# The first two attention blocks with queries on partitions, and a float64 conversion whose sign is carried by Prelu

## The chip, the cores and the metric

The kernel runs on one core of a Trainium2 chip. The metric is device time in microseconds (us), the median of several executions. The profile is of one execution; its engines are PE (matrix products), DVE (vector), ACT (scalar functions), POOL, and SP, which here issues the DMAs.

## The reference, cut to what matters

Attention with a causal mask and a bias from cumulated sums, then two feed-forward blocks, the first behind a layer norm and the second behind a mixing of rank 32 along the sequence. Batch 4, 8 heads, sequence S = 576, head size 64, width 512, hidden width 2048. The weights of both feed-forward blocks, U and V come in float64.

```python
# attention, per batch and head
cum  = cumsum(maximum(s, 0), -1)
bias = -(cum[..., :, None] - cum[..., None, :])
scores = where(causal, -1e9, q @ k.T / 8 + minimum(bias, 0))
attn = exp(scores - max(scores)); attn = attn / (sum(attn) + 1e-9)
x = attn @ v                                   # (B, S, 512) over all heads
# first feed-forward block
xn = (x - mean(x)) / sqrt(var(x) + 1e-6) * g_ln
x = x + maximum(xn @ w_ch1, 0) @ w_ch2
# second: mix along the sequence, then feed-forward
u = x + (x.T @ U @ V).T
out = u + maximum(u @ w_ch1b, 0) @ w_ch2b
```

## The kernel before, in words

Rows of the sequence are worked on in blocks: A is queries 0 to 255 and B queries 256 to 575 of a batch; A0 is block A of batch 0, B3 block B of batch 3. For each block attention runs by pairs of heads (class `Pair`, four pairs per block): `load`, `prep` (split into a high and a low part), `score`, `trans` (the probabilities are transposed on PE, copied to a tile `pB`) and `pv`. A0 and A1 (`FULL`) use full float32 and no split. In `score` a matmul with `sel` and `ksum` adds the bias, DVE takes the maximum in the same pass in which it masks (L761), ACT takes the exponential with a running sum (L767, an activation and then a read of its accumulator), a reciprocal follows (L774), and the probabilities are multiplied by it on ACT, DVE or POOL (L780 to L783). `pv` (L846 for the full blocks) has v as the stationary operand, so its result has the head's 64 features on partitions; it is copied into the block's tile x (L374 or L375), 128 features of 512 by 256 queries.

`layer_norm` then works on x with features on partitions: sums over features are products with a tile of ones (L920 and L927), everything else is passes of 128 by 256. Its result is split in `xh` and `xl`, the operands of the feed-forward matmuls. A block of the first feed-forward layer takes 16 steps, each for 128 hidden units (`mlp1` at L1277 to L1279, `mlp2` at L1310 to L1312). Steps 0 to 7 are A0 with the first half of the hidden units, 8 to 15 A1 with the same weights, 16 to 31 both with the second half. 128 such steps are followed by the second layer.

Weights come as pairs of 32-bit words in a raw tile `wr` (four of them). `f64_to_f32` makes float32 of them in four operations: ACT scales the high words (L507), ACT turns the low words into integers (L511), DVE shifts and joins them (L513), DVE puts the sign in from the raw tile (L515). The result is split in a high and a low part. Steps 0 to 7 split into `w` tiles (`w_split`) and write them out; the second half is converted ahead and written out (`w_ahead`, from step `W0`), and is loaded again later; the second layer's weights likewise (`w1_ahead`, `w2_ahead`, from step `W1`).

Order: every operation is handed to a planner (`Plan`) with a priority and an estimated cost for each engine that can do it. The planner simulates the engines and one DMA queue, does four more passes with due times and prices, keeps the shortest, and writes the order out. Buffers of a tag are given out in the order in which they were asked for. `AT` says between which steps a block's attention is asked for, `LN` at which step its layer norm. Until the first matmul of step 0 the planner fills PE's waits with matmuls on ones (L1463, fillers). `setup` loads s, cumulates it and builds `ksum`, the sums relative to the last key of each range, for 128, 256, 384 and 512 keys, and the 576-key sums that go to memory (L433 to L449).

Of the kernel before, what the change touches and what calls it, by code (L numbers as in the profile page):

```python
# [41 lines left out]
def f(ap):  # L42
    return ap.bitcast(F32)
# [285 lines left out]
def mha_ffn_mixer_ffn(ctx: ExitStack, tc, qkv_p, qkv_a, qkv_b, s, g, w1, w2, U, V, out):  # L329
# [70 lines left out]
    COL = [sum(KEYS[:i]) for i in range(5)]  # L400
# [11 lines left out]
    def setup():  # L412
        s_sb, cum = (P.buf("pB", [128, 2, 1344]) for _ in range(2))

        def rel(c0, c1):
            return s_sb.tile.rearrange("p a c -> p (a c)")[:, c0:c1]

        for y in range(4):
            load(PRO, R * S * 4, lambda y=y: nc.sync.dma_start(s_sb[R * y:R * (y + 1), 0, :S], s), [], [(s_sb, "y%d" % y)])
# [9 lines left out]
        def mask(d, n):  # L429
# [3 lines left out]
        dve(PRO, S, lambda: nc.vector.tensor_scalar(out=s_sb[:, 0, :S], in0=s_sb[:, 0, :S], scalar1=0.0, scalar2=8.0, op0=ALU.max, op1=ALU.mult),  # L433
            [s_sb], [s_sb], 0.521)
        dve(PRO, S, lambda: nc.vector.tensor_tensor_scan(cum[:, 0, :S], s_sb[:, 0, :S], s_sb[:, 0, :S], 0.0, ALU.add, ALU.max),
            [s_sb], [cum], 1.042)

        for i in range(5):
            c0, c1 = COL[i], COL[i] + KEYS[i]
            pr = PRO + (i >= 2)  # L440
            dve(pr, KEYS[i], lambda i=i, c0=c0, c1=c1: nc.vector.tensor_scalar(
                out=rel(c0, c1), in0=cum[:, 0, :KEYS[i]], scalar1=cum[:, 0, KEYS[i] - 1:KEYS[i]], scalar2=None, op0=ALU.subtract),
                [cum] + [s_sb] * (i == 0), [s_sb] if i == 0 else [(s_sb, i)], 0.521, 128)
            if i == 4:
# [54 lines left out]
    def f64_to_f32(prio, n, dst, raw, bd, br, words=(0, 1), psum=False):  # L499
# [108 lines left out]
    class Pair:  # L608
# [11 lines left out]
        def load(self, prio, gate):  # L620
# [93 lines left out]
        def score(self, prio, tick):  # L714
# [7 lines left out]
            rd = [qk] if full else [(qk, x) for x in ("raw", "h", "l")] if self.blk == "A" else [(qk, x) for x in ("kh", "kl", "k", "qh", "ql", "z0", "z1", "q0", "q1", "q2")]  # L722
            nt = len(tick)
            nc_ = len(ts) * nt
            sm, rc = (P.buf(tag, [128, 4]) for tag in ("sm", "rc"))
# [18 lines left out]
            else:  # L744
                for x, i in enumerate(tick):
# [13 lines left out]
                    pe(prio - 500, 1.2 * mm_full(K) + mm_cost(K) if full else 4 * mm_cost(K) + 200, mm, rd + [sel, (ksum, i)], [(ps, x) for ps in pss], ts)  # L759
# [73 lines left out]
        def pv(self, prio, z):  # L833
# [10 lines left out]
            def mm_f():  # L844
                for k, (j, o0, o1, c) in enumerate(mms):
# [668 lines left out]
```

## Time and profile before

| | |
|---|---|
| runs | 1067.99, 1072.34, 1072.24 us, median 1072.24 |
| profiled execution | 1071.02 us, span of its instructions 1069.2 us |
| busy share of the span | PE 97%, DVE 66%, ACT 48%, POOL 16% |
| mean granted clock of PE | 0.996 of full speed |
| moved by DMA | 253.58 MB, mean 237 GB/s |

PE's busy time counts the fillers too, and an average over the span mixes stages with different limits. Rows of a view give a group's instructions as count, busy time and mean length of one; a granted clock of 1.00 is 2.4 GHz and 0.50 is 1.2 GHz. Window rows give busy time by engine with the number of instructions in brackets, then the granted clock, the DMA share and GB/s.

### The profile page before, as it was taken

Reading aid. Unit: us, or ns where it says so; the run is one execution under the profiler, and the core shown is the slowest. Engines: PE = TensorE matmul, PEld = TensorE weight load, DVE = VectorE, ACT = ScalarE, POOL = GpSimd, SP = SyncE. Lnnn points to the kernel's source line nnn. Section 1 sums busy time; section 2 is a strip of 40 time slices with the busy share of each in tenths; the row PEclk is TensorE's granted clock in tenths of the full one; section 3 lists DMA queues with packets and bytes.
Section 4 is the critical chain, followed back from the end, with each engine's and each line's share of the span. In section 5 each row is a group of like instructions: output and inputs, shape, how many; then the busy total and the mean of one; then the engine's idle time right before and its main releaser. Section 6 shows DMA issues by size and latency. Waiting matters only on the chain.

```text
span 1069.2 us, 20135 instructions
## 1 busy us (share of the span) xinstructions
PE 1042.1 (97%) x7393; PEld 960.0 (90%) x7393; DVE 709.3 (66%) x1744; ACT 508.5 (48%) x1224; POOL 175.5 (16%) x333
## 2 busy tenths in 40 slices
PE   9998999999999999989999999999999999999998
PEld 6687998999999999979899999999998999899997
DVE  7999978886798766685785533755645744744521
ACT  7988866785676564575664332421211311311211
POOL 1123213241341232211420000200100200200000
PEclk9998999999999999999999999999999999999999
DMA  6999997555954598378349599995474375176483
GB/s 231 356 327 330 335 363 258 187 177 204 324 170 147 187 325 271 122 236 301 113 162 332 194 333 404 340 342 204 149 268 165 109 276 196 54 249 230 138 276 100
DMA packets 98755, 253.58 MB, mean 237 GB/s; under 512 B 16320, under 2 KB 44992, under 8 KB 94304
## 3 DMA queue, kind: packets, MB, share of 16 engines
q1 hardware_dynamic: 98656, 252.28, 68.4%
q8 instruction: 59, 0.97, 0.4%
q14 instruction: 40, 0.33, 0.1%
HBM read 198.69 MB, written 62.99 MB: 245 GB/s over the span
## 4 chain that ended last, share of the span: by engine, by line
PE 70%; DMA 11%; DVE 8%; ACT 6%; issue 2%; SPq 1%; POOL 1%; DVEq 0%; ACTq 0%; POOLq 0%
PE ps L1199 5%; PE ps L1201 5%; PE ps L1200 5%; PE ps L1277 5%; PE ps L1279 4%; PE ps L1278 4%; PE acc L1310 3%; PE acc L1312 3%; PE acc L1311 3%; PE acc L1236 3%; PE acc L1237 3%; PE ps L1236 3%; PE ps L1237 3%; PE acc L1238 3%; PE ps L1238 3%; PE ps L853 3%
## 5 line engine op out<-in xcount | busy, mean ns | idle before, releaser
L1277 PE MATMUL ps<-xh,w 128*128 128x256 f32 (+1 forms) x512 | 160.5, 314 | 3.3 <-DVE mx L761 1.9
L1279 PE MATMUL ps<-xl,w 128*128 128x256 f32 (+1 forms) x512 | 152.5, 298 | 1.2 <-POOL xl L381 1.2
L1278 PE MATMUL ps<-xh,w 128*128 128x256 f32 (+1 forms) x512 | 152.4, 298 | 0.0
L1310 PE MATMUL acc<-hh,w 128*128 128x256 f32 (+1 forms) x448 | 136.6, 305 | 0.5 <-ACT hh L1283 0.5
L1312 PE MATMUL acc<-hl,w 128*128 128x256 f32 (+1 forms) x448 | 130.1, 290 | 0.6 <-DVE hl L1284 0.6
L1284 DVE SCALAR_TENSOR_TENSOR hl<-ps,hh 128x256 fp32r<-128x256 f32 (+1 forms) x144 | 64.6, 449 | 98.6 <-ACT hh L1283 97.9
L1311 PE MATMUL acc<-hh,w 128*128 128x256 f32 (+1 forms) x448 | 129.9, 290 | 0.0
L1283 ACT ACTIVATE hh<-ps 128x256 fp32r<-128x256 f32 (+1 forms) x144 | 57.7, 403 | 118.5 <-PE ps L1279 117.9
L1277 PEld LDWEIGHTS ps<-xh,w 128*128 128x128 f32 x512 | 98.1, 192 | 9.3 <-issue 2.7
L1279 PEld LDWEIGHTS ps<-xl,w 128*128 128x128 f32 x512 | 97.8, 191 | 1.5 <-POOL xl L381 1.5
L1278 PEld LDWEIGHTS ps<-xh,w 128*128 128x128 f32 x512 | 98.2, 192 | 0.7
L767 ACT ACTIVATE t<-t,mx 128x128 f32<-128x128 f32 (+4 forms) x144 | 83.0, 578 | 29.2 <-DVE mx L761 20.9
L1159 ACT ACTIVATE w<-hl 128x256 fp32r<-128x256 f32 x87 | 35.5, 417 | 124.2 <-DVE hl L1179 124.1
L1310 PEld LDWEIGHTS acc<-hh,w 128*128 128x128 f32 x448 | 85.2, 190 | 3.4 <-issue 1.8
L1312 PEld LDWEIGHTS acc<-hl,w 128*128 128x128 f32 x448 | 85.1, 190 | 1.1 <-DVE hl L1284 1.1
L1311 PEld LDWEIGHTS acc<-hh,w 128*128 128x128 f32 x448 | 85.3, 191 | 0.3
L1179 DVE TENSOR_TENSOR hl<-ps,hh 128x256 f32<-128x256 f32 x128 | 48.6, 418 | 45.0 <-PE ps L1201 43.9
L1179 DVE TENSOR_TENSOR hh<-ps,hh 128x256 f32<-128x256 f32 x64 | 27.1, 423 | 73.1 <-ACT hh L374 71.9
L806 PE MATMUL ps<-ident,t 128*128 128x128 f32 x400 | 64.5, 277 | 10.5 <-ACT t L780 3.2
L379 DVE TENSOR_TENSOR pB<-ps,pB 128x512 fp32r<-128x512 f32 (+1 forms) x112 | 62.6, 571 | 14.3 <-ACT pB L374 13.6
L374 ACT ACTIVATE pB<-ps 128x384 fp32r<-128x384 f32 (+3 forms) x115 | 56.5, 500 | 18.7 <-PE ps L806 18.0
L806 PEld LDWEIGHTS ps<-ident,t 128*128 128x128 f32 x400 | 46.3, 140 | 18.9 <-ACT t L780 5.4
(235 smaller groups left out, 2847.9 us busy)
## 6 DMA issues: line engine op xcount, KB each, us to landing
w<-w_dr SPq DMA_DIRECT2D x128, 512.0 KB, 7.4
pB<-w_dr SPq DMA_DIRECT2D x34, 1024.0 KB, 6.2
w_dr<-wr SPq DMA_DIRECT2D x48, 512.0 KB, 4.7
qk<-w_dr SPq DMA_DIRECT2D x26, 768.0 KB, 5.9
wr<-w1a SPq DMA_DIRECT2D x16, 512.0 KB, 5.8
wr<-w2a SPq DMA_DIRECT2D x16, 512.0 KB, 6.4
w_dr<-w SPq DMA_DIRECT2D x16, 512.0 KB, 6.4
wr<-w1b SPq DMA_DIRECT2D x16, 512.0 KB, 6.5
```

The lines of the kernel that those rows point to most:

```text
L767: act(prio, K, lambda t=t, mx=mx, o=o, K=K, x=x, y=nt * z + x: nc.scalar.activation(t[:, o:o + K], t[:, o:o + K], AF.Exp, bias=mx[:, (1 if ...
L806: nc.tensor.transpose(ps[:, 128 * j:128 * (j + 1)], t[:, c:c + 128], ident.tile)
L1179: dve(st - 1000, 256, lambda: nc.vector.tensor_tensor(out=d.tile, in0=region(r), in1=a.tile, op=ALU.add), [p, a], [d])
L1236: nc.tensor.matmul(aa[z].tile, w[:, 0, sl], h[:, 0], start=first, stop=False)
L1237: nc.tensor.matmul(aa[z].tile, w[:, 1, sl], h[:, 0], start=False, stop=False)
L1277: nc.tensor.matmul(ps[:, :n], lhs(k, 0), xh[:, k, :n], start=k == 0, stop=False)
L1278: nc.tensor.matmul(ps[:, :n], lhs(k, 1), xh[:, k, :n], start=False, stop=False)
L1279: nc.tensor.matmul(ps[:, :n], lhs(k, 0), xl[:, k, :n], start=False, stop=k == KT - 1)
L1284: dve(st - 1000, n, lambda: nc.vector.scalar_tensor_tensor(out=hl[:, :n], in0=ps[:, :n], scalar=0.0, in1=f(hh[:, :n]), op0=ALU.max, op1=AL ...
L1310: nc.tensor.matmul(a, w[:, 0, sl], hh[:, :n], start=new, stop=False)
L1311: nc.tensor.matmul(a, w[:, 1, sl], hh[:, :n], start=False, stop=False)
L1312: nc.tensor.matmul(a, w[:, 0, sl], hl[:, :n], start=False, stop=last and (z == 1 or blk == "B"))
```

## The change

For A0 and A1 the product with v is turned (`pv_tok`): the transposed probabilities, now not normalised, are the stationary operand, and v with 64 columns of ones beside it is the moving one. The result has queries on partitions, with the sum of each query's probabilities in the 64 columns beside it. One reciprocal and one multiply normalise it into a tile of 128 queries by 2 by 512. The running sum in the exponential, the pass over the probabilities and the copies of x by head go. The layer norm (`layer_norm_tok`) takes mean and variance along the free axis with statistics operations, scales, and eight transposes bring the normalised x to features on partitions, where g is multiplied in as it is split. x itself is brought to that form later (`x_columns`, at priorities 10 and 18: eight transposes and two copies for each block). `layer_norm` stays for all other blocks.

The tile of q, k, v holds two pairs and the columns of ones; q and k come in one load, v in another. `setup` first loads, cumulates and subtracts only 256 columns; the rest has priority 5. The range of 128 keys is dropped (it uses the 256-key sums). In `f64_to_f32` one Prelu on ACT scales positive words by 2^-112 and negative ones by -2^-80; the three-bit shift that follows moves that difference of exponents into the sign bit, and the sign step on DVE goes. Planner costs of the two ACT steps go from 94 to 135 ns besides the width, and `AT`, `LN`, `W0` and `W1` get other numbers.

```diff
--- before.py
+++ after.py
@@ -32,10 +32,10 @@
 LAST = ("C0", "C1", "C2", "C3", "T0")
 W2SLOTS = 12
 
-AT = {"A2": (6, 9), "A3": (12, 35), "B0": (26, 46), "B1": (48, 63), "B2": (67, 86), "B3": (76, 100)}
-LN = {"A2": 18, "A3": 35, "B0": 55, "B1": 63, "B2": 86, "B3": 100}
-W0 = (4, 12)
-W1 = (16, 66, 50)
+AT = {"A2": (3, 11), "A3": (6, 35), "B0": (24, 46), "B1": (48, 59), "B2": (67, 84), "B3": (78, 98)}
+LN = {"A2": 15, "A3": 35, "B0": 59, "B1": 61, "B2": 84, "B3": 98}
+W0 = (0, 8)
+W1 = (10, 72, 50)
 PASSES = 4
 
...
@@ setup
+        sc, cum = P.buf("xc", [128, 1280]), P.buf("v", [128, 1280])
+        late = 5
+        part = ((0, 256, PRO), (256, S, late))
+
+        for c, (c0, c1, pr) in enumerate(part):
+            for y in range(4):
+                load(pr, R * (c1 - c0) * 4, lambda y=y, c0=c0, c1=c1: nc.sync.dma_start(sc[R * y:R * (y + 1), c0:c1], s[:, c0:c1]), [], [(sc, ("s", c))])
...
+        for c, (c0, c1, pr) in enumerate(part):
+            k = (sc, ("s", c))
+            dve(pr, c1 - c0, lambda c0=c0, c1=c1: nc.vector.tensor_scalar(out=sc[:, c0:c1], in0=sc[:, c0:c1], scalar1=0.0, scalar2=8.0, op0=ALU.max, op1=ALU.mult),
+                [k], [k], 0.521)
+            dve(pr, c1 - c0, lambda c0=c0, c1=c1: nc.vector.tensor_tensor_scan(
+                cum[:, c0:c1], sc[:, c0:c1], sc[:, c0:c1], cum[:, c0 - 1:c0] if c0 else 0.0, ALU.add, ALU.max),
+                [k] + [(cum, 0)] * c, [(cum, c)], 2.084)
+
+        REL = {1: (sc, 576), 2: (sc, 832), 3: (sc, 0), 4: (cum, 640)}
+        for i, (a, c) in REL.items():
             c0, c1 = COL[i], COL[i] + KEYS[i]
-            pr = PRO + (i >= 2)
...
@@ f64_to_f32
-        alts = {"act": (94 + 0.8333 * n, lambda: nc.scalar.activation(dst(), pair(1), AF.Copy, scale=2.0 ** -112))}
...
+        act(prio, n, lambda: nc.scalar.activation(dst(), pair(1), AF.Prelu, scale=2.0 ** -112, alpha=-2.0 ** 32), [(br, words[1])], [bd], 135)
...
-        dv(lambda: nc.vector.scalar_tensor_tensor(out=dst().bitcast(U32), in0=pair(1).bitcast(U32), scalar=0x80000000,
-                                                  in1=dst().bitcast(U32), op0=ALU.bitwise_and, op1=ALU.bitwise_or), [bd, (br, words[1])], [bd])
@@ Pair.load
-                qk = self.qk = self.v = P.buf("qk", [128, 768], dt)
-                load(prio, 512 * 768, lambda: nc.sync.dma_start(qk.tile, qkv_p[b, p]), [], [qk], gate)
+                if p % 2 == 0:
+                    qk = self.qk = P.buf("qk", [128, 2, 832], dt)
+                    P.op(prio, {"pool": (200, lambda: nc.gpsimd.memset(qk[:, :, 768:], 1.0))}, [], [(qk, "one")])
+                else:
+                    qk = self.qk = pairs_of[b, blk][p - 1].qk
+                for c0, c1, key in ((0, 512, "qk"), (512, 768, "v")):
+                    load(prio, 512 * (c1 - c0), lambda c0=c0, c1=c1: nc.sync.dma_start(qk[:, p % 2, c0:c1], qkv_p[b, p, :, c0:c1]), [], [(qk, (key, p % 2))], gate)
...
@@ Pair.score
+                    if full:
+                        act(prio, K, lambda t=t, mx=mx, o=o, K=K, x=x: nc.scalar.activation(
+                            t[:, o:o + K], t[:, o:o + K], AF.Exp, bias=mx[:, x:x + 1], scale=-1.0), [(t, i), (mx, x)], [(t, i)], 160)
+                        continue
...
+            if full:
+                return
...
+        def pv_tok(self, prio):
+
+            b, p, pT, qk = self.b, self.p, self.pT[0], self.qk
+            ps = psum()
+            mms = [(i, z, j) for i in range(2) for z in range(2) for j in range(i + 1)]
+
+            def vv(z, j):
+                c = 512 + 64 * (2 * z + j)
+                a = qk[:, p % 2, c:c + 64]
+                return bass.AP(tensor=a.tensor, offset=a.offset, ap=[a.ap[0], (768 - c, 2), (1, 64)])
+
+            def mm():
+                for k, (i, z, j) in enumerate(mms):
+                    c = 128 * (2 * i + z)
+                    nc.tensor.matmul(ps[:, c:c + 128], pT[:, z, 128 * (i + j):128 * (i + j + 1)], vv(z, j), start=k == 0, stop=k == len(mms) - 1)
+
+            pe(prio - 500, 6 * mm_full(128), mm, [pT, (qk, ("v", p % 2)), (qk, "one")], [ps])
+            if (b, "tok") not in xt:
+                xt[b, "tok"] = P.buf("x", [128, 2, DM])
+            x, sm, rc = xt[b, "tok"], P.buf("sm", [128, 4]), P.buf("rc", [128, 4])
+
+            def reg():
+                return ps.tile.rearrange("p (i z c) -> p i z c", i=2, z=2)
+
+            dve(prio, 4, lambda: nc.vector.tensor_scalar(out=sm.tile, in0=ps.tile.rearrange("p (a c) -> p a c", a=4)[:, :, 64], scalar1=1e-9, scalar2=None, op0=ALU.add),
+                [ps], [sm])
+            dve(prio, 7, lambda: nc.vector.reciprocal(rc.tile, sm.tile), [sm], [rc])
+
+            def norm():
+                r = rc.tile
+                r4 = bass.AP(tensor=r.tensor, offset=r.offset, ap=[r.ap[0], (2, 2), (1, 2), (0, 64)])
+                nc.vector.tensor_tensor(out=x[:, :, 128 * p:128 * (p + 1)].rearrange("p i (z c) -> p i z c", z=2), in0=reg()[..., :64], in1=r4, op=ALU.mult)
+
+            dve(prio, 256, norm, [ps, rc], [(x, p)])
...
+                    if pr.full:
+                        items.append((800, lambda p, g, pr=pr: pr.pv_tok(p)))
+                    for z in () if pr.full else range(2):
...
+    def to_columns(prio, src, reads, k0):
+        ps = psum()
+
+        def tr():
+            for k in range(k0, k0 + 2):
+                for i in range(2):
+                    nc.tensor.transpose(ps[:, 256 * (k - k0) + 128 * i:256 * (k - k0) + 128 * (i + 1)], src(i)[:, 128 * k:128 * (k + 1)], ident.tile)
+
+        pe(prio - 500, 4 * 109, tr, reads + [ident], [ps])
+        return ps
+
+    def layer_norm_tok(prio, b):
+        x, w = xt[b, "tok"], P.buf("ls", [128, 320])
+        n = [P.buf("xs", [128, DM]) for _ in range(2)]
+
+        def st(i, c):
+            return w[:, 12 * i + 6 * c:12 * i + 6 * (c + 1)]
+
+        def col(c):
+            return w[:, 32:36].rearrange("p (i c) -> p i c", i=2)[:, :, c]
+
+        mean, var, y, z = lambda i: w[:, 32 + 2 * i:33 + 2 * i], lambda: col(1), lambda: w[:, 40:42], lambda: w[:, 48:50]
+        for c in range(2):
+            for i in range(2):
+                dve(prio, 256, lambda i=i, c=c: nc.vector.bn_stats(out=st(i, c), in_=x[:, i, 256 * c:256 * (c + 1)]), [(x, 2 * c), (x, 2 * c + 1)], [(w, (i, c))])
+        for i in range(2):
+            dve(prio, 12, lambda i=i: nc.vector.bn_aggr(out=w[:, 32 + 2 * i:34 + 2 * i], in_=w[:, 12 * i:12 * (i + 1)]), [(w, (i, 0)), (w, (i, 1))], [(w, ("mv", i))])
+        mv = [(w, ("mv", i)) for i in range(2)]
+        act(prio, 2, lambda: nc.scalar.activation(y(), var(), AF.Ln, bias=eps.tile), mv + [eps], [(w, "y")], 145)
+        act(prio, 2, lambda: nc.scalar.activation(y(), y(), AF.Exp, scale=-0.5), [(w, "y")], [(w, "y")])
+        dve(prio, 2, lambda: nc.vector.scalar_tensor_tensor(out=z(), in0=var(), scalar=1e-6, in1=y(), op0=ALU.add, op1=ALU.mult), mv + [(w, "y")], [(w, "z")])
+        dve(prio, 2, lambda: nc.vector.tensor_tensor(out=z(), in0=z(), in1=y(), op=ALU.mult), [(w, "y"), (w, "z")], [(w, "z")])
+        dve(prio, 2, lambda: nc.vector.scalar_tensor_tensor(out=y(), in0=z(), scalar=-3.0, in1=y(), op0=ALU.add, op1=ALU.mult), [(w, "y"), (w, "z")], [(w, "y")])
+        for i in range(2):
+            dve(prio, DM, lambda i=i: nc.vector.tensor_scalar(out=n[i].tile, in0=x[:, i], scalar1=mean(i), scalar2=w[:, 40 + i:41 + i], op0=ALU.subtract, op1=ALU.mult),
+                [x, mv[i], (w, "y")], [n[i]], 0.521, 128)
+        xh, xl = P.buf("xh", [128, KT, 320], F32R), P.buf("xl", [128, KT, 320], F32R)
+        for k0 in (0, 2):
+            ps = to_columns(prio, lambda i: n[i], n, k0)
+            for k in range(k0, k0 + 2):
+                def half(k=k, ps=ps, k0=k0):
+                    return ps[:, 256 * (k - k0):256 * (k - k0 + 1)]
+
+                P.op(prio, {
+                    "act": (144 + 0.8333 * 256, lambda k=k, half=half: nc.scalar.activation(xh[:, k, :256], half(), AF.Copy, scale=g_sb[:, k:k + 1])),
+                    "dve": (128 + 1.042 * 256, lambda k=k, half=half: nc.vector.tensor_scalar(out=xh[:, k, :256], in0=half(), scalar1=g_sb[:, k:k + 1], scalar2=None, op0=ALU.mult)),
+                }, [ps, g_sb], [(xh, k)])
+                dve(prio, 256, lambda k=k, half=half: nc.vector.scalar_tensor_tensor(
+                    out=xl[:, k, :256], in0=half(), scalar=g_sb[:, k:k + 1], in1=f(xh[:, k, :256]), op0=ALU.mult, op1=ALU.subtract),
+                    [ps, g_sb, (xh, k)], [(xl, k)], fixed=128)
+        xn[0, b, "A"] = (xh, xl)
+
+    def x_columns(prio, b):
+        t = xt.pop((b, "tok"))
+        x = xt[b, "A"] = P.buf("x", [128, KT, 256])
+        for k0 in (0, 2):
+            ps = to_columns(prio, lambda i: t[:, i], [t], k0)
+            copy(prio, 512, lambda k0=k0: x[:, k0:k0 + 2, :], lambda ps=ps: ps.tile.rearrange("p (k c) -> p k c", k=2), [ps], [(x, k0)], psum=True)
...
-    layer_norm(-50, 0, "A")
+    layer_norm_tok(-50, 0)
     for _, fn in attn_items(1, "A"):
         fn(1, None)
-    layer_norm(4, 1, "A")
+    layer_norm_tok(4, 1)
+    for b in range(2):
+        x_columns(10 + 8 * b, b)
     w_next(0, None)
     w_next(1, None)
     for k in range(2 * WSLOTS):
```

## Rows read from the trace of the kernel before

**Rows 1.** Windows: PE, PEld, DVE, ACT, POOL busy; clock, DMA share, GB/s.

```profile
0.00:9.70 9.70, 8.60 (x54) 6.35 (x54) 5.34 (x14) 4.06 (x10) 1.48 (x8) 1.00 0.70 228
9.70:50.60 40.90, 37.31 (x279) 26.40 (x279) 37.50 (x109) 36.81 (x107) 6.64 (x15) 1.00 0.84 304
50.60:92.20 41.60, 38.70 (x311) 33.86 (x309) 39.87 (x107) 38.61 (x106) 9.03 (x20) 1.00 0.97 337
92.20:126.00 33.80, 31.23 (x248) 29.72 (x248) 31.09 (x78) 28.08 (x76) 11.20 (x20) 0.90 0.92 318
126.00:200.00 74.00, 71.18 (x604) 67.77 (x601) 60.37 (x165) 51.59 (x139) 19.36 (x40) 1.00 0.88 304
200.00:1069.20 869.20, 855.08 (x5910) 795.94 (x5908) 535.09 (x1274) 349.31 (x792) 127.78 (x231) 1.00 0.64 221
```

**Rows 2.** Timeline of PE: start, length, instruction, idle time before it and releaser.

```profile
9.69 0.33 PE L753 MATMUL ps<-ksum,sel 64*128 64x128 f32 x2
...
24.86 2.14 PE L1463 MATMUL acc<-ones 128*128 128x256 bf16 x18
...
50.65 0.36 PE L1277 MATMUL ps<-xh,w 128*128 128x256 f32 x1
...
92.23 0.58 PE L1277 MATMUL ps<-xh,w 128*128 128x256 f32 x1 [0.55 <-ACT xh L374]
```

**Rows 3.** The fillers' line: count, length in ns, first and last start.

```profile
L1463 PE MATMUL acc<-ones x173: 272/273/418, 1.1 to 50.6; 128*128 128x256 bf16 x173
```

**Rows 4.** One window, columns as in Rows 1.

```profile
90.00:100.00 10.00, 7.85 (x39) 7.22 (x40) 9.56 (x20) 8.77 (x25) 6.81 (x11) 0.66 0.85 310
```

**Rows 5.** Groups on DVE, 9.7 to 92.2 us: count, busy us, mean ns.

```profile
L515 DVE SCALAR_TENSOR_TENSOR ps<-wr,ps 128x512 uint32<-128x512 uint32 x21 | 14.2, 687 | 0.1
...
L940 DVE TENSOR_TENSOR xc<-x,ps 128x256 f32<-128x256 f32 x8 | 2.8, 415 | 0.0
L375 DVE CAST w<-ps 128x512 fp32r<-128x512 f32 x4 | 2.8, 688 | 0.1
...
L963 DVE SCALAR_TENSOR_TENSOR xc<-xc,g_sb,ls 128x256 f32<-128x256 f32 x4 | 1.7, 477 | 0.0
L774 DVE RECIPROCAL rc<-sm 128x4 f32<-128x4 f32 x9 | 1.6, 173 | 0.6 <-POOL sm L772 0.4
```

**Rows 6.** Groups on ACT, the same stretch.

```profile
L767 ACT ACTIVATION_READ_ACCUMULATOR t<-t,mx 128x1 f32 x40 | 7.6, 190 | 0.0
...
L374 ACT ACTIVATE x<-ps 64x256 f32<-64x256 f32 x15 | 5.6, 370 | 1.3 <-PE ps L846 1.1
...
L780 ACT ACTIVATE t<-t,rc 128x256 f32<-128x256 f32 x8 | 3.9, 495 | 0.0
...
L780 ACT ACTIVATE t<-t,rc 128x128 f32<-128x128 f32 x7 | 2.5, 392 | 0.0
```

**Rows 7.** Timeline of DVE, in setup and in A0's layer norm.

```profile
4.21 0.46 DVE L433 TENSOR_SCALAR pB<-pB 128x576 f32<-128x576 f32 x1 [3.16 <-DMA pB<-s]
...
4.70 1.36 DVE L435 TENSOR_TENSOR_SCAN pB<-pB 128x576 f32<-128x576 f32 x1
...
40.63 1.41 DVE L940 TENSOR_TENSOR xc<-x,ps 128x256 f32<-128x256 f32 x4
```

**Rows 8.** Pieces of the chain that ended last: start, length, what.

```profile
57.00 0.33 PE ps L806 x3
...
78.04 1.46 PE ps L846 x8
```

**Rows 9.** Waits, SP's queue to 200 us and PE's: total us, times, longest.

```profile
SPq L524 <- DVE ps L515: 16.2, 8, 6.7
...
PE ps L757 <- DMA qk<-qkv_p: 1.2, 2, 0.9
```

**Rows 10.** Timeline of ACT at the start.

```profile
0.75 1.28 ACT L1466 ACT_TABLE_LOAD   x1 [0.75 <-PEq L1507]
```

**Rows 11.** Issues of second-layer w1 loads: length ns, first and last start.

```profile
L524 SPq DMA_DIRECT2D wr<-w1b x16: 327/437/947, 153.0 to 655.3; - x16
```

More of the change, by code (lines that the diff above doesn't have):

```diff
@@ L399, in mha_ffn_mixer_ffn @@
     KEYS = [min(128 * (i + 1), S) for i in range(5)]
-    COL = [sum(KEYS[:i]) for i in range(5)]
+    COL = [sum(KEYS[1:i]) for i in range(5)]
+    COL[0] = COL[1]
     ksum = fixed("ksum", [128, COL[4]], F32R)
@@ new lines, in setup, with rel @@
+        REL = {1: (sc, 576), 2: (sc, 832), 3: (sc, 0), 4: (cum, 640)}
+        for i, (a, c) in REL.items():
+            c0, c1 = COL[i], COL[i] + KEYS[i]
+            pr = PRO if i == 1 else late
+            key = [(a, ("s", y)) for y in range(2)] if i == 3 else [(a, 10 + i)]
+            def rel(y0=0, y1=4, a=a, c=c, i=i):
+                return a[R * y0:R * y1, c:c + KEYS[i]]
+            dve(pr, KEYS[i], lambda i=i, rel=rel: nc.vector.tensor_scalar(
+                out=rel(), in0=cum[:, :KEYS[i]], scalar1=cum[:, KEYS[i] - 1:KEYS[i]], scalar2=None, op0=ALU.subtract),
+                [(cum, y) for y in range(1 + (i > 1))], key, 0.521, 128)
@@ L444, in setup @@
             if i == 4:
-                load(pr, R * S * 4, lambda: nc.sync.dma_start(cum_dr.tile, rel(COL[4], COL[4] + S)[:R]), [(s_sb, 4)], [cum_dr])
+                load(pr, R * S * 4, lambda rel=rel: nc.sync.dma_start(cum_dr.tile, rel(0, 1)), key, [cum_dr])
                 break
-            act(pr, KEYS[i], lambda c0=c0, c1=c1: nc.scalar.activation(ksum[:, c0:c1], rel(c0, c1), AF.Copy), [(s_sb, i)], [(ksum, i)])
+            act(pr, KEYS[i], lambda c0=c0, c1=c1, rel=rel: nc.scalar.activation(ksum[:, c0:c1], rel(), AF.Copy), key, [(ksum, i)])
@@ L673, in qkt @@
         def qkt(self, r, u, c0, c1):
-            return self.qk[r, c0:c1] if self.full else self.qk[r, u, c0:c1]
+            return self.qk[r, self.p % 2 if self.full else u, c0:c1]
         def prep(self, prio):
@@ L721, in score @@
             ranges = [(0, 288), (288, S)] if last else [None]
[L722 removed]
+            rd = [(qk, ("qk", self.p % 2))] if full else [(qk, x) for x in ("raw", "h", "l")] if self.blk == "A" else [(qk, x) for x in ("kh", "kl", "k", "qh", "ql", "z0", "z1", "q0", "q1", "q2")]
             nt = len(tick)
             nc_ = len(ts) * nt
[L725 removed]
+            sm, rc = (None if full else P.buf(tag, [128, 4]) for tag in ("sm", "rc"))
             mxs = [P.buf("mx", [128, 2]) for _ in ts]
@@ L842, in pv @@
             v0 = self.nj * z
-            def mm_f():
-                for k, (j, o0, o1, c) in enumerate(mms):
-                    nc.tensor.matmul(ps[:64, o0:o1], self.vt(v0 + j, None), pT[0][:, z, c:c + o1 - o0],
-                                     start=k == 0, stop=k == len(mms) - 1)
             def mm():
@@ L868, in pv @@
             copy(prio, n, dst, lambda: ps[:64, :n], [ps], [(x, h)], psum=True)
-            if not self.full:
-                dve(prio, n, lambda: nc.vector.tensor_tensor(out=dst(), in0=ps[64:, :n], in1=dst(), op=ALU.add), [ps, (x, h)], [(x, h)])
+            dve(prio, n, lambda: nc.vector.tensor_tensor(out=dst(), in0=ps[64:, :n], in1=dst(), op=ALU.add), [ps, (x, h)], [(x, h)])
+        def pv_tok(self, prio):
[24 more added lines that the diff above has]
+            dve(prio, 256, norm, [ps, rc], [(x, p)])
     pairs_of = {(b, blk): [Pair(b, p, blk) for p in range(H // 2)] for b in range(B) for blk in BLK}
@@ L902, in attn_items @@
                 if (n - 1) % per == per - 1:
-                    for z in range(2):
+                    if pr.full:
+                        items.append((800, lambda p, g, pr=pr: pr.pv_tok(p)))
+                    for z in () if pr.full else range(2):
                         items.append((400, lambda p, g, pr=pr, z=z: pr.pv(p, z)))
@@ L912, in mha_ffn_mixer_ffn, with ln_sum @@
     xn = {}
-    xf = {}
-    def ln_sum(prio, n, srcs, reads, into, full=False):
-        if full:
-            ps = psum()
-            for k in range(KT):
-                pe(prio - 500, mm_full(n), lambda k=k: nc.tensor.matmul(ps[:, :n], ones.tile, srcs[k](), start=k == 0, stop=k == KT - 1),
-                   [ones] + reads[k], [ps])
-            return ps
+    def ln_sum(prio, n, srcs, reads, into):
         for k in range(1, KT):
@@ L944, in layer_norm @@
             sq.append(q)
-        var = ln_sum(prio, n, [lambda q=q: q[:, :n] for q in sq], [[q] for q in sq], sq[0], head)
-        for k in range(0 if head else KT):
+        var = ln_sum(prio, n, [lambda q=q: q[:, :n] for q in sq], [[q] for q in sq], sq[0])
+        for k in range(KT):
             P.op(prio, {
```

44 lines of the change are left out of this document (8 added, 36 removed).

## The prediction

> **What bounds the kernel now.** I read the profile by stretches first, then the order of PE's work, then the costs inside the slow stretches, and last the transfers.
>
> The stretches [rows 1] fall into two parts. From 200 us on PE is busy 855 of 869 us while DVE has a third of its time free: there only PE's own work counts. Before that DVE and ACT are the full engines: between 9.7 and 92.2 us DVE is busy 77.4 and ACT 75.4 of 82.5 us, and the DMA share goes from 0.84 to 0.97. PE's share in those rows misleads, for some of it is filler. The order of PE's work shows two gates [rows 2]: the first score at 9.69 us, the first matmul of MLP step 0 at 50.65 (block A0's layer norm is the last thing before it), and the first of step 8, the first step of block A1, at 92.23, released by A1's own layer norm. Fillers [rows 3] are 173 matmuls up to 50.6 us, eighteen of which stand in 2.14 us, so about 0.11 each and 19.0 us or more in all. Of PE's 84.6 busy us before 92.2 at most 65.6 are work, and 26.6 us of that stretch are waste. That waste, and 2.6 us of idle PE from there to 126 us, is what a change to the first two blocks can win. The low clock belongs to it: 0.66 between 90 and 100 us [rows 4], so 1.2 GHz for most of it, after the gaps around A1's layer norm; 0.34 of 7.85 busy us is 2.7 us, of which I take 2.
>
> **The change, part by part.** Terms for DVE and ACT between 9.7 and 92.2 us, from [rows 5, 6].
>
> Removed. The sign step: 21 x 0.687 = 14.4 us of DVE. The normalising pass over the probabilities on ACT: 8 x 0.495 + 7 x 0.392 = 6.7 (POOL's share of that pass costs nothing, POOL is busy under a quarter of the time). The accumulator reads behind the exponentials: 40 x 0.190 = 7.6 at most, nothing at least if they hide behind the neighbour; I take half, 3.8. Fifteen copies of PV out of PSUM on ACT: 15 x 0.370 = 5.6. The two layer norms: up to 92.2 us they make 46 passes of 128x256 on DVE and ACT, of which the eight subtractions are the largest group on DVE at 0.415; at 0.40 they are 18.4. Sum 48.9.
>
> Added. Each of eight pairs: one multiply out of PSUM over 256 columns (0.415, as the subtraction, which also reads PSUM) and one add on four sums (0.173, as the reciprocal; the reciprocal itself stays): 8 x 0.59 = 4.7. Each token layer norm: four statistics passes, which the trace does not have; the nearest rows bound them by 0.173 (a tiny operation) and 0.688 (a copy of 512), and I take 0.415, a pass of the same width, 1.7; two aggregations and five tiny operations at 0.173, 1.2; two scalings of 512 at 0.688 or less, 1.4; four copies out of PSUM at 0.370, 1.5; four subtractions at 0.477, 1.9: 7.7, and 15.4 for two (13.4 to 17.6 by the bounds). The return of x to columns: two copies of 512 per block at 0.688, 2.8 for both. Sum 22.9. The sums over 384 to 576 keys move from before the first score to later in the same stretch or were there already; I count them at nothing, and at 2 us if all of them are new to it.
>
> Net 26.0 us less for two engines, 13.0 each if the planner evens them out. Neighbours overlap: four subtractions of 0.415 take 1.41 in a row instead of 1.66 [rows 7], so 13.0 x 0.85 = 11.0.
>
> The start. Before the first score lie a relu of 0.46 from 4.21 us and a scan of 1.36, both over 576 columns [rows 7], then subtractions for every key range: 5.5 us from 4.21 to 9.69. Over 256 columns the first two are about 0.2 and 0.6; one subtraction (0.3), one copy on ACT (0.4) and two partial subtractions (0.4 each) follow, with 0.7 of hand-overs: 3.0 us, estimates by width. Saved 2.5. So step 8 may start at 92.2 - 2.5 - 11.0 = 78.7, 13.5 us earlier.
>
> PE. PV has the same columns as before (1.46 us for a pair [rows 8], 768 columns either way), but loads 128 stationary columns in place of 64; the trace does not show that form. Least zero, most another half of 1.46 per pair, 6 us; as most pairs lie where fillers stand now I take zero. Transposes take 0.33 us for three [rows 8]: the first block's eight for the layer norm fall among the fillers; the second block's eight and the sixteen that return x come to 2.6 us of PE, less four records of ones-matmuls in A1's layer norm at 1.46/8 each: 1.9 us that nothing hides.
>
> What is late next: the transfers. The first 16 weight tiles, for steps 0 to 7, serve step 8 again, but step 16 (around 126 us) wants the second half of the layer's weights, converted, written out and read back, and the DMA engines were nearly full all that time. Their idle shares up to 126 us [rows 1]: 0.30 x 9.7 + 0.16 x 40.9 + 0.03 x 41.6 + 0.08 x 33.8 = 2.9 + 6.5 + 1.2 + 2.7 = 13.3 us. The first two, 9.4 us, can be filled: the queue waited 16.2 us for the sign step before it could load into the next raw tile [rows 9], and that step was the tile's last reader. I let the transfers pass 9.4 of the 13.5 us, and PE returns 1.9: 7.5 us gained. Span 1069.2 - 7.5 = 1061.7; the profiled execution took 1071.0, 1.8 us over its span, so 1063.5. It lies within the three runs shown (1068.0 to 1072.3), 1.2 under their median.
>
> Costed at nothing: the sign steps outside this stretch (64 weight tiles in all, 43 of them here, 30 us of DVE). Most lie after 200 us under PE's full time, where DVE has a third free; were PE not the bound, up to 30 us. Also at nothing: the deeper loads of q, k, v, two pairs per buffer and two loads per pair in place of one, so eight more issues on SP's queue, and four more for the later columns of s; the first score waited for the sums and not for them, and if that cover is gone it costs one landing, 1.2 us as PE waited for them in all before [rows 9].
>
> Prelu has no row. The copy that it replaces is one strided pass over 512 elements; between nothing and a tiny ACT operation more (0.190, the accumulator read) I take nothing, as the shape stays; 0.19 x 21 = 4 us of ACT would bring 2 us back.
>
> The ACT table is loaded once, 1.28 us at the start [rows 10]. The Trainium skill (ScalarE: Activation LUTs, Table sets: the hidden batching unit) says that a function outside the loaded set costs a load at every switch, which speaks against a new function between exponentials and copies. The trace agrees on what one load takes, and nothing in it says which set Prelu is in.
>
> **The rivals.**
>
> *Transfers do not bind* (0.18). PE has attention of the later blocks to do while weights come, and write-backs may wait. Then all 13.5 us arrive, the gap at 92 us closes with its clock loss of 2, PE returns 1.9: 13.6 less, 1055.6 + 1.8 = 1057.4. For it: PE waited little for DMA, 1.2 us in the longest such entry [rows 9]. Against: a DMA share of 0.92 to 0.97 from 50.6 us on.
>
> *Only the start is kept* (0.24). The order is written out by a planner from estimated costs; if the chains of short operations wait on latencies instead of engine time, and later gates stay, 2.5 - 1.9 = 0.6 us: 1068.6 + 1.8 = 1070.4, no change. For it: A0's layer norm took from its subtractions at 40.63 us [rows 7] to 50.65, far longer than its operations. Against: what it queues behind, weights and scores, is what shrinks.
>
> *The layer-2 weights collide* (0.12, slower). Their preparation may begin at step 10 instead of 16. The first w1 pair (six transfers' worth of 0.5 MB) and two w2 tiles (four) are ten, 5.24 MB, at the 337 GB/s of the stretch [rows 1] 15.6 us of DMA. If they go ahead of the second-half weights on SP's queue, PE waits that long before step 16 and the clock falls again (2): 1069.2 - 7.5 + 15.6 + 2 + 1.8 = 1081.1. It turns the sign once more than 7.5 us of such waits stand there. Against: their first load now comes at 153.0 us [rows 11], some 27 us after its gate opens, so the planner puts it behind urgent loads.
>
> *Prelu is in another table* (0.02, slower): two loads of 1.28 around each of about 32 conversions up to 126 us, 82 us on a full ACT: beyond 1110.
>
> **How the numbers follow.** The forecast itself (0.44) spans 1059 to 1067 by the bounds of statistics, reads and Prelu, some 4 us. About 0.5% (5 us) is what a measurement of this kernel tells from no change: faster means below 1066.9, slower above 1077.6. Faster is the forecast and the first rival, 0.62; same 0.24; slower 0.14. The range 1054 to 1074 leaves out the slower cases and a few of the widest.
>
> **What would show it.** The first score near 7 us; no sign step, 44 us less DVE for the 64 tiles; step 0 near 42 us and step 8 near 79; fewer than 173 fillers; a DMA share above 0.9 between 10 and 50 us; step 16 some 9 us earlier; no second table load. Wrong would make it: step 8 still near 90, PE waiting for reloaded weights between 100 and 140 us, or a gain up to 126 us that is lost again by 200 us as idle PE.

## The result, and the profile after

The changed kernel takes 1057.47 us (median of 4 runs, 1056.54 to 1059.89) against 1071.57 before (four runs: the three shown above and 1070.90): ratio 0.987, 95% interval 0.985 to 0.990. It is faster by 14 us. The forecast was 1063.5 with a range of 1054 to 1074, so the time lies in it, nearer to the rival "transfers do not bind" (1057.4) than to the forecast.

Windows of the changed kernel, with the same bounds and columns as [rows 1]:

```profile
0.00:9.70 9.70, 8.57 (x62) 7.00 (x63) 2.94 (x7) 5.93 (x12) 1.72 (x10) 1.00 0.78 273
9.70:50.60 40.90, 38.78 (x338) 31.63 (x336) 34.91 (x113) 36.28 (x82) 0.41 (x2) 1.00 0.96 337
50.60:92.20 41.60, 40.63 (x354) 38.92 (x353) 38.07 (x113) 34.45 (x90) 5.66 (x10) 1.00 0.97 339
92.20:126.00 33.80, 33.80 (x300) 32.81 (x299) 27.65 (x79) 24.74 (x71) 5.34 (x12) 1.00 0.98 356
126.00:200.00 74.00, 72.16 (x594) 67.83 (x593) 60.44 (x168) 53.83 (x142) 20.66 (x40) 1.00 0.92 300
200.00:1055.80 855.80, 844.25 (x5832) 788.81 (x5831) 512.23 (x1233) 334.84 (x760) 117.05 (x216) 1.00 0.64 221
```

Up to 126 us PE now idles 4.2 us (126 less the first four busy times) against 10.2 before, and after 126 us 13.4 against 16.9. The clock is full in every stretch; the window that had 0.66 before [rows 4] has this row:

```profile
90.00:100.00 10.00, 10.00 (x97) 9.46 (x97) 9.54 (x32) 7.22 (x22) 3.13 (x5) 1.00 0.92 312
```

PE's timeline, the places of [rows 2]: the first score, the first matmul of step 0, the last before step 8, step 8, and step 16. The first row is fillers.

```profile
10.81 10.42 PE L1552 MATMUL acc<-ones 128*128 128x256 bf16 x94
22.14 0.78 PE L761 MATMUL ps<-ksum,sel 64*128 64x128 f32 x2 [0.91 <-DVE ksum L459]
...
51.25 0.36 PE L1364 MATMUL ps<-xh,w 128*128 128x256 f32 x1
...
86.91 0.49 PE L820 MATMUL ps<-ident,t 128*128 128x128 f32 x3
87.16 0.36 PE L1364 MATMUL ps<-xh,w 128*128 128x256 f32 x1
...
116.44 0.36 PE L1364 MATMUL ps<-xh,w 128*128 128x256 f32 x1
```

Step 16 in the kernel before:

```profile
127.15 0.47 PE L1277 MATMUL ps<-xh,w 128*128 128x256 f32 x1
```

The fillers' line, as [rows 3], and PE's time in fillers up to step 0 (busy PE, busy weight load, clock, DMA share, GB/s), changed and before:

```profile
L1552 PE MATMUL acc<-ones x205: 272/273/421, 1.1 to 49.3; 128*128 128x256 bf16 x103
...
0.00:51.25 51.25, 25.84 (x205) 20.82 (x205) 1.00 0.93 326
```

```profile
0.00:50.65 50.65, 24.18 (x173) 17.35 (x173) 1.00 0.81 290
```

This is not the course that was forecast. The first score comes 12 us later than before, not 2.5 us earlier; there are more fillers, not fewer; step 0 starts 0.6 us later. Step 8 comes 5.1 us earlier, and no idle time stands before it any more, where 0.55 us for A1's layer norm stood. Starts of further steps, each read from PE's timeline (us):

| step | before | changed | difference |
|---|---|---|---|
| 0 | 50.65 | 51.25 | +0.6 |
| 8 | 92.23 | 87.16 | -5.1 |
| 16 | 127.15 | 116.44 | -10.7 |
| 32 | 193.21 | 181.79 | -11.4 |
| 48 | 272.63 | 262.13 | -10.5 |
| 96 | 539.64 | 525.82 | -13.8 |
| end of span | 1069.2 | 1055.8 | -13.4 |

So most of the gain is made between step 0 and step 16, some 3 us of it after step 48. The head of ACT's, DVE's and SP's timelines shows what the planner did with the shorter attention:

```profile
0.75 0.40 SPq L420 DMA_DIRECT2D xc<-s  x1
...
1.21 0.41 SPq L529 DMA_DIRECT2D wr<-w1a  x1
...
4.87 0.64 ACT L517 ACTIVATE ps<-wr 128x512 f32<-128x512 f32 x1 [1.88 <-DMA wr<-w1a]
...
12.43 0.42 SPq L420 DMA_DIRECT2D xc<-s  x1
...
18.70 0.29 DVE L436 TENSOR_SCALAR xc<-xc 128x256 f32<-128x256 f32 x1
```

Weights are loaded and converted first; the fourth quarter of s is asked for at 12.43 us and the relu runs at 18.70. A0's attention starts 12 us later and still ends in time for step 0, with more weight tiles already done: 15 conversions have begun by 50.6 us instead of 11, and from 9.7 to 50.6 us DMA is busy 0.96 of the time instead of 0.84. PE then finds both steps and attention of later blocks to do.

The new operations on DVE and ACT, groups between 9.7 and 80 us (columns as in [rows 5, 6]):

```profile
L1046 DVE SCALAR_TENSOR_TENSOR xl<-ps,g_sb,xh 128x256 fp32r<-128x256 f32 x8 | 3.3, 476 | 0.1
L908 DVE TENSOR_TENSOR x<-ps,rc 128x256 f32<-128x256 f32 x8 | 3.2, 415 | 0.1
L1023 DVE BATCH_NORM_STATS2 ls<-x 128x6 f32<-128x256 f32 x8 | 3.1, 416 | 0.1
...
L1033 DVE TENSOR_SCALAR xs<-x,ls 128x512 f32<-128x512 f32 x4 | 2.0, 543 | 0.0
...
L901 DVE TENSOR_SCALAR sm<-ps 128x4 f32<-128x4 f32 x8 | 1.3, 157 | 1.0 <-PE ps L891 0.9
...
L517 ACT ACTIVATE ps<-wr 128x512 f32<-128x512 f32 x18 | 11.5, 636 | 1.7 <-DMA wr<-w1a 1.6
...
L1043 ACT ACTIVATE xh<-ps,g_sb 128x256 fp32r<-128x256 f32 x7 | 2.7, 469 | 0.0
L374 ACT ACTIVATE x<-ps 128x512 f32<-128x512 f32 x4 | 2.4, 592 | 0.0
```

Prices were right where a row was near: statistics 0.416 (0.415 taken), the multiply out of PSUM 0.415 (0.415), the split 0.476 (0.477), the add on four sums 0.157 (0.173). Prelu takes 0.636 us, the copy at the same place before took 0.634. The scaling of 512 and the copies of x are cheaper than the 0.688 taken (0.543 and 0.592), and only the scaled copy out of PSUM is dearer, 0.469 instead of 0.370.

### The profile page after: what moved, and what is told of

Read it like the earlier page. It is cut to its first block, busy times and chain, and to the rows that moved or that the text cites. A ratio compares the mean times of both kernels' runs of the same rounds, so it can differ in the third digit from the quotient of the medians.

```text
span 1055.8 us, 20049 instructions
## 1 busy us (share of the span) xinstructions
PE 1038.2 (98%) x7469; PEld 967.0 (92%) x7469; DVE 676.2 (64%) x1709; ACT 490.1 (46%) x1152; POOL 150.8 (14%) x289
## 4 chain that ended last, share of the span: by engine, by line
PE 78%; DVE 7%; DMA 6%; ACT 4%; issue 1%; SPq 0%; POOL 0%; DVEq 0%; ACTq 0%; POOLq 0%
PE ps L1364 6%; PE ps L1366 5%; PE ps L1365 5%; PE ps L1286 5%; PE ps L1288 5%; PE ps L1287 5%; PE acc L1397 4%; PE acc L1399 4%; PE acc L1398 4%; PE ps L862 3%; PE ps L820 3%; PE acc L1323 3%; PE acc L1324 3%; PE ps L1323 3%; PE ps L1324 3%; PE acc L1325 3%
## 5 line engine op out<-in xcount | busy, mean ns | idle before, releaser
L1364 PEld LDWEIGHTS ps<-xh,w 128*128 128x128 f32 x512 | 97.0, 189 | 4.3 <-DVE hl L1371 1.1
L1365 PEld LDWEIGHTS ps<-xh,w 128*128 128x128 f32 x512 | 97.1, 190 | 0.6
L779 ACT ACTIVATE t<-t,mx 128x384 f32<-128x384 f32 (+4 forms) x112 | 68.9, 618 | 28.6 <-DVE mx L769 25.4
L1266 DVE TENSOR_TENSOR hh<-ps,hh 128x256 f32<-128x256 f32 x64 | 27.1, 423 | 76.1 <-ACT hh L374 74.8
L374 ACT ACTIVATE pB<-ps 128x512 fp32r<-128x512 f32 (+3 forms) x119 | 59.1, 502 | 25.5 <-PE ps L820 25.2
L374 ACT ACTIVATE hh<-ps 128x256 f32<-128x256 f32 x31 | 11.9, 384 | 109.7 <-PE ps L1288 109.6
```

What stands on the lines that cost most here:

```text
L374: "act": ((51 if psum else 94) + 0.8333 * n, lambda: nc.scalar.activation(out(), a(), AF.Copy)),
L1266: dve(st - 1000, 256, lambda: nc.vector.tensor_tensor(out=d.tile, in0=region(r), in1=a.tile, op=ALU.add), [p, a], [d])
L1364: nc.tensor.matmul(ps[:, :n], lhs(k, 0), xh[:, k, :n], start=k == 0, stop=False)
L1365: nc.tensor.matmul(ps[:, :n], lhs(k, 1), xh[:, k, :n], start=False, stop=False)
```

## The experiments

Three theories stood against each other. *Sign*: the DVE time of the sign step, and its hold on the raw tiles, make the gain. *Layout*: the shorter attention and layer norm of A0 and A1 make it. *Plan*: the planner's new numbers make it. Two kinds of kernel tell them apart: those planned anew, and those in which the planned order is kept and only what is emitted differs. Ratios are to the kernel before, run on the same chip; there it took 1071.6 to 1072.8 us, so a difference between two runs of different chips can be off by 1 us from that alone.

**The sign step left out of the order before** (e1_nosign).

```diff
-        dv(lambda: nc.vector.scalar_tensor_tensor(out=..., in0=pair(1)..., scalar=0x80000000, ...), [bd, (br, words[1])], [bd])
+        dv(lambda: None, [bd, (br, words[1])], [bd])
```

> The kernel before, its planned order and all planner costs kept, but the sign step on DVE is not emitted: the weights' signs are left out. The only difference is that 67 DVE passes of 0.69 us are gone and that the raw tile's last reader is the shift step. Theory 'sign' (the step's DVE time and its hold on the raw tiles make most of the gain): 5 to 10 us less than before, step 8 before 89 us. Theory 'layout' (the shorter attention and layer norm of A0 and A1 make it) and theory 'plan' (the planner's new numbers make it): within 3 us of before.

1065.66 us, ratio 0.993 (0.992 to 0.995): 6.5 us less. The step is worth something, but not where I had put it: step 8 starts at 91.0, 1.2 earlier, step 16 at 125.0 (2.2), step 32 at 190.0 (3.2), step 64 at 349.3 (5.1 of the 354.5 before), step 112 at 599.1 (7.7). Two thirds of the gain come after step 16. Its step 16:

```profile
124.95 0.47 PE L1276 MATMUL ps<-xh,w 128*128 128x256 f32 x1
```

**The sign step without its hold on the raw tile** (e2_signconst).

```diff
-  in0=pair(1).bitcast(U32), scalar=0x80000000
+  in0=causal[:, :n].bitcast(U32) if psum and n == 512 else pair(1).bitcast(U32), scalar=0x80000000
```

> The kernel before, order kept, the sign step emitted on DVE with the same width, but with a constant tile in place of the raw tile as input, so the weights' signs are wrong. DVE time is as before; only the raw tile is free one DVE pass earlier. The same order without the step took 6.5 us less (1065.7). If the hold on the raw tiles makes that: 4 to 7 us less than before. If DVE's time makes it: within 2 us of before.

1072.44 us, ratio 1.000 (0.998 to 1.001). The queue's wait for the sign step [rows 9] is gone from this trace, but the DMA share from 9.7 to 50.6 us only rises from 0.84 to 0.86, step 16 starts 1.0 us earlier, and at the end nothing is left. So the hold is worth nothing that the runs can tell, within some 2 us; what e1_nosign won is DVE's time.

```profile
9.70:50.60 40.90, 37.61 (x286) 27.06 (x286) 38.17 (x111) 37.58 (x111) 7.01 (x16) 1.00 0.86 311
```

**The conversion alone, planned anew** (e3_prelu_only, and e8_prelu_94 with the old cost of its two ACT steps).

```diff
 # before.py, f64_to_f32
+  act(prio, n, lambda: nc.scalar.activation(dst(), pair(1), AF.Prelu, scale=2.0 ** -112, alpha=-2.0 ** 32), ..., 135)   # e8: no 135
-  (the copy and the sign step)
```

> The kernel before with the new conversion alone (Prelu, no sign step, the new planner costs of the two ACT steps), planned anew; attention, layer norm, setup, AT, LN, W0 and W1 as before. Theory 'sign': 8 to 13 us less than before. Theory 'layout': 0 to 4 us less. Theory 'plan': within 4 us of before.

> The kernel before with the new conversion alone, as in e3_prelu_only, but with the planner's old cost (94 ns besides the width) for both ACT steps, planned anew. With 135 it came to 0 although the same step left out of the kept order took 6.5 us. If the costs made the planner lose it: 1064 to 1068. If any new order of this layout loses it: 1069 to 1074.

With 135: 1072.82 us, ratio 1.001 (1.000 to 1.003), nothing. With 94: 1066.92 us, ratio 0.996 (0.993 to 0.998). The operations are the same in both; the planner's estimate differs, and by it the order and the choice of engine where there is one (1752 instructions on DVE in the first, 1696 in the second). In the first, step 32 is 3.9 us ahead of the kernel before and step 64 4.0 behind.

**The layout alone, planned anew** (e4_tok_only), the changed kernel with the old conversion.

> The changed kernel with the old conversion (ACT copy, sign step on DVE, the old planner costs), planned anew; everything else as changed. Theory 'sign': within 4 us of before, so 10 to 14 above the changed kernel. Theory 'layout': 8 to 13 us less than before, within 5 of the changed kernel. Theory 'plan': 4 to 12 us less than before.

1066.37 us, ratio 0.996 (0.994 to 0.997): 5.8 us less, between what *layout* and *sign* had said and inside the 4 to 12 of *plan*. This kernel has the new numbers and the narrow start of `setup` as well, and it is one planned order; how much of the 5.8 is layout is taken up below.

**The same without the sign step, order kept** (e10_tok_nosign; the edit of e1_nosign in that kernel).

> The kernel of e4_tok_only (new layout, old conversion, 1066.4), its planned order and costs kept, the sign step not emitted (the weights' signs are left out). If the two parts simply add, the step is worth the same 6.5 us as in the kernel before: 1058.5 to 1061.5. If with the new layout DVE binds more, so that both parts are needed together: below 1058. If the new layout has already taken the waits: above 1063.

1060.33 us, ratio 0.989 (0.985 to 0.993): 6.0 us below e4_tok_only, in the range for parts that simply add. About 6 each, 12 together, within the interval of this run, some 4 us to either side.

**The numbers AT, LN, W0, W1** (e5_after_oldconst: the changed kernel with the old ones; e6_before_newconst: the kernel before with the new ones).

> The changed kernel with AT, LN, W0 and W1 of the kernel before, planned anew. The two parts alone came to 0 (conversion) and 5.8 us less (layout) than before, both together to 14. Theory 'plan' (the missing 8 us are the numbers tuned to both parts): 1063 to 1068. Theory 'both parts are needed' (each frees one of DVE and ACT, and the fuller one binds): 1056 to 1061.

> The kernel before with AT, LN, W0 and W1 of the changed kernel alone, planned anew. Theory 'plan': 3 us or more below before. Theory 'both parts are needed': within 3 us of before, or slower.

1061.99 us, ratio 0.991 (0.988 to 0.995), between the two ranges, and 1073.30 us, ratio 1.001 (0.999 to 1.003). Alone the numbers are worth nothing, against *plan*. With both parts they are worth 4.5 us by the medians, but the intervals overlap, so that is not shown. What they do to the course is plain. Step 8 in e5_after_oldconst, then in e6_before_newconst:

```profile
78.70 0.28 PE L1364 MATMUL ps<-xh,w 128*128 128x256 f32 x1
```

```profile
100.78 0.52 PE L1277 MATMUL ps<-xh,w 128*128 128x256 f32 x1
```

In either layout the new numbers put step 8 back by 8.5 us (78.70 to 87.16, 92.23 to 100.78), for attention of A2 and A3 is asked for earlier: between step 0 and step 8 of the changed kernel stand 32 score matmuls of L765, in e5_after_oldconst 8. Step 16 is put back by less, 2.0 and 1.4 us.

**Sums over 576 keys first** (e11_sums576).

```diff
-        part = ((0, 256, PRO), (256, S, late))
+        part = ((0, S, PRO),)
-            pr = PRO if i == 1 else late
+            pr = PRO if i == 1 else PRO + 1
```

> The changed kernel with the sums over all 576 keys first, as before (one load of s per quarter, one relu, one scan; the subtractions for the larger ranges right behind), planned anew; all else as changed. The prediction gave the narrow start 2.5 us. As the first score of the changed kernel stands at 22 us behind conversions, the start should bind nothing: within 3 us of the changed kernel, 1055 to 1061. If it is worth what was predicted: 1060 or more.

1060.35 us, ratio 0.989 (0.986 to 0.993): 2.9 us above the changed kernel, the intervals overlapping. It lies at the edge of both expectations and settles nothing about the narrow start; its step 8, at 86.9 us, is where it was.

**The sign step put back, order kept** (e7_sign_back).

```diff
-        dv(lambda: (shift step), [bd, (br, words[0])], [bd])
+        def join(): (shift step); (sign step of the kernel before)
+        dv(join, [bd, (br, words[0]), (br, words[1])], [bd])
```

> The changed kernel, its planned order and costs kept, with the old sign step emitted behind the shift step inside the same planned operation (Prelu stays, so it changes no value): 67 DVE passes of 0.69 us are back and hold the raw tile. Theory 'both parts are needed' with DVE time as the cost: 6 us or more above the changed kernel, with PE idle coming back before step 16. Theory 'layout' or 'plan': less than 3 us above it.

1091.57 us, ratio 1.019 (1.016 to 1.021): 34 us above the changed kernel for 46 us of DVE, and 25 above e4_tok_only, in which the planner knew of the same step. Its windows:

```profile
9.70:50.60 40.90, 33.47 (x280) 27.67 (x278) 36.37 (x103) 30.16 (x64) 0.41 (x2) 0.96 0.85 280
50.60:92.20 41.60, 36.13 (x312) 32.63 (x313) 39.38 (x121) 30.49 (x78) 2.47 (x4) 1.00 0.82 288
92.20:126.00 33.80, 31.39 (x259) 30.32 (x258) 30.03 (x73) 25.17 (x71) 6.29 (x13) 0.95 0.91 313
```

DVE is busy 89 to 95% of the time, ACT in the first two windows and DMA in all three are less busy than in the changed kernel, and PE idles 15.3 us: most of its long waits are for DVE. The longest single wait of PE before 130 us is for the first sums, queued behind conversions:

```profile
PE ps L766 <- DVE ksum L459: 3.8, 1, 3.8
```

**Fewer bytes, order kept** (e12_halfback).

```diff
-  nc.sync.dma_start(dr[:, half], f(w.tile))            # write-back of a first-half tile
+  nc.sync.dma_start(dr[:, half, 0], f(w.tile)[:, 0])
-  nc.sync.dma_start(f(w.tile), dr[:, half])            # every reload
+  nc.sync.dma_start(f(w.tile), twice(dr[:, half, 0]))  # the same 256 KB read twice
```

> The changed kernel, its order and costs kept, but the write-backs of the first 16 weight tiles carry only the high parts, 0.25 MB each instead of 0.5, and later reloads take the high part twice (the low parts of the weights are wrong). 4.2 MB less, some 12 us of DMA before step 16. If the transfers set when steps 0 to 16 come: 3 us or more below the changed kernel, step 16 before 114 us. If DVE, ACT and the planned order set it: within 2 us of the changed kernel.

1081.10 us, ratio 1.009 (1.007 to 1.012), 24 us above the changed kernel; neither expectation. As a whole it is no test, for the reloads changed too: the same bytes come in rows of half the length. Its head is one, for its first reload is asked for at 99.8 us. Windows and the DMA totals, with those of the changed kernel last:

```profile
9.70:50.60 40.90, 39.12 (x337) 31.55 (x335) 35.28 (x114) 36.93 (x82) 0.41 (x2) 1.00 0.91 304
50.60:92.20 41.60, 40.89 (x357) 39.10 (x357) 38.06 (x113) 34.56 (x92) 6.04 (x11) 1.00 0.86 289
...
DMA packets 112384, 249.36 MB, mean 231 GB/s; under 512 B 16512, under 2 KB 46464, under 8 KB 107936
...
w<-w_dr SPq DMA_DIRECT2D x128, 512.0 KB, 8.9
```

```profile
DMA packets 100096, 253.55 MB, mean 240 GB/s; under 512 B 16512, under 2 KB 46464, under 8 KB 95648
...
w<-w_dr SPq DMA_DIRECT2D x128, 512.0 KB, 7.5
```

Between 9.7 and 92.2 us the DMA share falls from 0.96 and 0.97 to 0.91 and 0.86, PE's busy time rises by 0.6 us, and step 16 starts at 115.8 instead of 116.4. Transfers that are done sooner move nothing there in this order. The changed kernel's own trace agrees: its first reload is issued 15 us before step 16, the six issued up to 117 us landed after 6.0 to 11.3 us, and PE waits for none of them.

```profile
101.32 1.03 SPq L550 DMA_DIRECT2D w<-w_dr  x1
...
DMA to landing us min/median/max: 6.0/8.2/11.3
```

**The old cost in the changed kernel** (e9_after_94), since 94 had been better in e8_prelu_94.

> The changed kernel with the planner's old cost (94 ns besides the width) for both ACT steps of the conversion, planned anew; the instructions are the same. In the kernel before, with the conversion alone, 94 in place of 135 took 5.9 us off (1072.8 to 1066.9). If the old cost is better for the order as such: 1050 to 1054. If 135 hurt only that one order, as one throw of the planner against another: 1055 to 1064, no better than the changed kernel.

1063.48 us, ratio 0.992 (0.990 to 0.993): 6 us worse than the changed kernel. The better cost of one layout is the worse one of the other.

## Why the prediction was right, and where its steps failed

**Right: the stretch and the direction.** Waste of PE (idle time, fillers, low clock) before step 16 was what the change could win, and 10.7 us of gain stand there at step 16. Of that waste most of the idle time went (10.2 to 4.2 us up to 126 us) and the 2.7 us of low clock; the fillers, its largest part, did not (24.18 and 25.84 us of PE). *Layout* and *sign* each give about 6 us (e4_tok_only; e1_nosign and e10_tok_nosign), and they add, as DVE's and ACT's terms did in the sum. The rest of the 14 us, some 2, is within the intervals; four orders of the changed operations or nearly the same (the changed kernel, e5, e9, e11) lie between 1057.5 and 1063.5, and the shipped one is the best of them.

The 5.8 us of *layout* are one order too. They are more than a throw because these four lie below all three kernels of the old layout without the sign step (e1, e8 and e3: 1065.7, 1066.9, 1072.8). The low clock belongs to *layout*: between 92.2 and 126 us the granted clock is 0.79 to 0.94 in all six kernels of the old layout, and 1.00 in all of the new but e7_sign_back (0.95). Here e1_nosign, then e4_tok_only:

```profile
92.20:126.00 33.80, 32.96 (x266) 31.55 (x267) 27.13 (x75) 27.95 (x78) 9.36 (x18) 0.91 0.95 323
```

```profile
92.20:126.00 33.80, 33.30 (x292) 31.96 (x291) 30.27 (x79) 25.11 (x74) 7.25 (x17) 1.00 0.99 359
```

The size was not right: the sum has 7.5 us and the span shrank by 13.4. The time lies inside because the range is 20 us wide.

**Failed: the start.** "The first score near 7 us" and "step 0 near 42 us" were wrong, because I let the order of the kernel before stand and shortened its operations. The planner works back from due times: shorter attention is started later, and the room goes to weights. The gain then shows as a denser PE from step 0 to 16 and not as an earlier step 0. Step 8 moved by 5.1 us, not 13.5, and that has a second cause: the sum left out `AT`, `LN`, `W0` and `W1`. With the old ones step 8 does start at 78.70 us (e5_after_oldconst), where the sum has 78.7. That is in part luck, for step 0 of that run starts at 50.20 and the start gave it 0.45 us, not 2.5. Step 8 is also no measure of the time: that kernel is no faster than the changed one. A smaller slip: the sum took all 40 accumulator reads of the stretch for A0's and A1's; 8 are not (the whole kernel had 144 and has 112).

**Failed: the transfers as the next bound.** I let 9.4 of 13.5 us pass because the DMA share was near full. e12_halfback frees DMA time up to 92 us and gains 0.7 us at step 16, and step 16 itself came 10.7 us earlier (12.7 in e5_after_oldconst). So the share was high because work was there, not because PE waited for it. Also wrong was the reason with which I let those 9.4 us pass, the sign step's hold on the raw tiles: e2_signconst puts it at nothing.

**Failed: the sign steps costed at nothing.** Of what leaving the step out gains in the kept order, about 4.5 of 6.5 us come after step 16, although DVE has a third free there. An average share does not say that a single pass hides. In all, idle PE falls from 27.1 to 22.0 us in that kernel (span less busy time), but 2.8 of these 5.1 us lie up to 126 us; so shorter waits of PE explain some half of what is won behind step 16. Which waits these are one by one, and where the other half comes from, I did not settle.

**The rivals.** The collision of second-layer weights did not come: PE is busy without a gap between 92.2 and 126 us. The ACT table is loaded once, so the Trainium skill's rule on switches (ScalarE: Activation LUTs, Table sets: the hidden batching unit) has nothing to bite on; that one table serves Prelu, Exp and Ln is shown by this row:

```profile
L1555 ACT ACT_TABLE_LOAD  x1: 1283/1283/1283, 0.7 to 0.7; - x1
```

"Only the start is kept" is out by size. "Transfers do not bind" had the time and its condition right; its course, a step 8 at 79 us, came only with the old numbers (e5_after_oldconst), so that its 1057.4 fits so well is in part luck.

**Open.** Why one order beats another by 6 us with the same operations (e3 against e8, e9 against the changed kernel) is not explained beyond that the gain of e3_prelu_only is lost between steps 32 and 64. What the narrow start is worth stays within that scatter (e11_sums576). Which part of the layout (attention, layer norm, the later return of x) gives its share was not tested.

## What to carry to other kernels

Where a planner writes the order, do not forecast times by shortening the old order: ask what it will put into the room, and look for the gain as density, not as an earlier start. To price one operation, keep the order and leave only its emission out; putting one back into an order planned without it prices it too high (34 us for the sign step here, against 6). To price a planner's number, run both values: here the scatter between orders, 6 us, is as large as either part of the change. A high DMA share is evidence of transfers, not of a wait for them; take bytes away and see whether a step moves.

## What the runs showed of the hardware

The product with v takes PE as long with 128 stationary columns as it took with 64: 1.50 us a pair in 12 instructions against 1.51 in 8, from the timelines of the changed kernel and of the kernel before.

```profile
53.48 1.50 PE L891 MATMUL ps<-qk,pB 128*128 128x128 f32 x12
```

```profile
20.64 1.51 PE L846 MATMUL ps<-pB,qk 128*64 128x256 f32 x8
```

A copy on ACT out of PSUM with a scale from a tile takes 0.469 us for 256 columns against 0.370 without (64 partitions); the Trainium skill (ScalarE: Activation LUTs, What ACT_TABLE_LOAD costs) gives about 93 ns for each such operand, and the 99 ns here agree. Reloads of 512 KB in rows of half the length took 8.9 us to land instead of 7.5 in the median, and the kernel with them was 24 us slower although it moved 4.2 MB less; that the reloads alone make those 24 us is not shown.
